# First MLP layer of the last two batches as a 2x2 block product with seven multiplications, placed behind attention

## The chip, the cores and the metric

The kernel runs on one core of a Trainium2 chip. The core has a matrix engine (TensorE, called PE in the profile), a vector engine (VectorE, DVE), an engine for activation functions (ScalarE, ACT), GpSimd (POOL) and an engine that mostly issues transfers (SyncE, SP). Each runs its own list of instructions in the written order and waits on semaphores for the others. Matrix products accumulate in PSUM (8 banks, each 512 fp32 wide in every partition); everything else lies in SBUF. The metric is the device time of one execution in microseconds; shown is the median of three runs.

## The reference

```python
def _attn_ref(q, k, v):                      # q, k, v: (8, 12, 448, 64)
    scores = scale * np.matmul(q, k.transpose(0, 1, 3, 2))
    attn = np.maximum(scores, 0.0) ** 2 / S
    return np.matmul(attn, v)
def _moe_ref(x, w_in, w_out):                # x: (3584, 768), w_in: (768, 2048), w_out: (2048, 768)
    h = x @ w_in
    g = 0.5 * h * (1.0 + erf(h * inv_sqrt2))
    return g @ w_out
# x is the attention output, heads side by side: 8 batches of 448 rows, 768 columns
```

So there are three parts: attention with squared ReLU for each batch and head, a first MLP layer with exact GELU, and a second MLP layer.

## The kernel before, in words

**Attention.** A batch has 12 heads in 3 groups `g` of 4. A QK step (`fn_qk`, L620) computes for one group 64 keys against 448 queries with four matmuls that use a quarter of the array each, into a PSUM buffer `ps` of two banks. A ReLU with scale brings it to bf16 in `a_sq`, on ACT (L632) or on DVE (L634), and DVE squares it (L641). Seven such steps make a group. Then an AV step (L680, 28 matmuls) multiplies with `v` into `pav`, and two copies (L384 on DVE, L386 on ACT) bring it to `xT`, the input of the MLP with features on partitions. `ps` and `pav` share a pool `w` of three two-bank buffers. An AV step is placed in the middle of the first four QK steps of the next group: two QK steps, the AV step, two QK steps, nothing else between them. The other three QK steps of a group stand together.

**First layer** (`add_f1`, L727). For each of 16 blocks `m` of 128 hidden units, six matmuls with a 128x128 weight tile of `win_sb` and 448 columns of `xT` accumulate in one PSUM bank of the pool `f` (two buffers); ACT applies GELU (L737) into the ring `h_sb`, which holds two batches. In batches 0 and 1 a few of these matmuls are 224 columns wide (half a batch).

**Second layer** (`add_group`, L834). Rows are taken in 14 groups of 256. The 2x2 block product (rows in two halves of 128, hidden units in two halves, output columns in two halves of 384) is formed with seven products instead of eight, of eight matmuls with 384 columns each. Four sums of `h_sb` blocks (L815, `s_sb`) and four differences of `wout_sb` blocks (L772, `t_sb`, made once by `add_tsums`) feed them; the partial results are added by DVE from PSUM (L868). The first 256 rows use plain products (`add_plain`, L929).

**Order.** The first 270 operations (attention of batches 0 and 1, the transposes, loads) follow a written list, `ORDER`. After it, the order on PE is fixed by the code at the end: for every batch `b` from 2 to 7 a stage of six slots takes the QK and AV steps, and between them "atoms" of the MLP. Stage `b` has the first layer of batch `b-1` and the groups that `GROUPS[b]` names, less the last three products of the last group, which are carried into the next stage (`CARRY`). So the stages hold different amounts of MLP work: two groups in stages 3, 4, 6 and 7, one in stages 2 and 5. Behind the attention of batch 7 come the rest of group 10, the first layer of batch 7, and groups 11 to 13. On ACT, DVE and SP a planner (`Scheduler`) chooses the order and, for ReLUs and copies, the engine, by its own costs, list positions and due times (`deadlines`).

**Transfers.** q and k of batches 2 to 7 are permuted by DVE (L463, L474) and transposed by seven transfers of the SP queue (L566 for kT, L575 for qT), which stand in one queue with the stores of the output rows (L795). POOL issues the loads; a small copy on POOL (`gate`, L587) waits for the transposes of batch `b+1` before the loads of `b+2` are issued. `wout_sb` is loaded in three pieces (L356).

Of the kernel before, what the change touches and what calls it, by code (L numbers as in the profile page):

```python
# [8 lines left out]
F32 = mybir.dt.float32  # L9
BF16 = mybir.dt.bfloat16  # L10
AF = mybir.ActivationFunctionType

B, H, S, D = 8, 12, 448, 64
# [37 lines left out]
SUM_BIAS = -0.3  # L51
TSUM_BIAS = 0.2
LEADS = {3: 8}
CARRY = 4
LAST = 256
PASSES = 2
NEAR = 0.5


def cols(half):  # L60
# [41 lines left out]
class Scheduler:  # L102
# [12 lines left out]
    def reset(self):  # L115
        self.free = {"PE": 6.0, "ACT": 2.6, "DVE": 1.0, "POOL": 1.25, "SP": 0.9}
        self.bufs = {name: [0.0] * n for name, n in self.buffers.items()}
        self.mode, self.dma = None, DMA_FREE
        self.landed = [0.0] * 8
        self.log = []  # L120
        for op in self.open:
            op.start = op.done = None

# [44 lines left out]
    def commit(self, est, op, eng, dur, lat):  # L168
        op.start = est
        if eng == "PE":  # L170
            self.mode = op.mode
            if est < self.COLD:
                dur, lat = 2 * dur, 2 * lat
        if isinstance(lat, tuple):
            t = max(self.dma, est + dur + 1.0)
            self.dma = t + lat[0] / 390e3
            op.done = self.dma + DMA_LAT
            self.landed += [op.done] * lat[1]
        else:
            op.done = est + lat  # L180
        self.free[eng] = est + dur
        for name in op.need:
            b = self.bufs[name]
            b[b.index(min(b))] = math.inf
        ends = [op.done] + [o.done for o in op.joint]
        if None not in ends:
            for name in op.frees:
                b = self.bufs[name]
                b[b.index(math.inf)] = max(ends)
        self.log.append((est, op, eng))  # L190

    def run(self, fixed):
# [11 lines left out]
    def deadlines(self):  # L204


        after = {id(o): [] for o in self.open}
        for o in self.open:
            for d in o.deps:
                if id(d) in after:  # L210
                    after[id(d)].append(o)
                elif isinstance(getattr(d, "op", None), Op):
                    after[id(d.op)].append(o)
        takers = {}
        for _, o, _ in self.log:
            for name in o.need:
                takers.setdefault(name, []).append(o)
        given = {}
        for _, o, _ in self.log:
            for name in o.frees:  # L220
                given.setdefault(name, []).append(o)
        for name, v in given.items():
            n = self.buffers[name]
            for x, o in enumerate(v):
                if x + n < len(takers[name]):
                    for y in [o] + list(o.joint):
                        after[id(y)].append(takers[name][x + n])
        self.late = {}
        t = math.inf
        order = sorted(self.log, key=lambda x: x[0])  # L230
        pe = [o for _, o, e in order if e == "PE"]
        ideal, at = {}, 0.0
        for o in pe:
            ideal[id(o)] = at
            at += o.engines[0][1]
        shift = pe[-1].start - ideal[id(pe[-1])]
        for est, o, e in reversed(order):
            t = ideal[id(o)] + shift if e == "PE" else est + 50.0
            for s in after[id(o)]:
                if id(s) in self.late:  # L240
                    t = min(t, self.late[id(s)] - (o.done - o.start))
            self.late[id(o)] = t

    def place(self, fixed):
# [36 lines left out]
def kernel(  # L281
# [100 lines left out]
    def copy(eng, dst, src):  # L382
        if eng == "DVE":
            V.tensor_copy(dst, src)  # L384
        else:
            A.copy(dst, src)  # L386

    def e_copy(n, psum=4):

        d = 0.07 + n / psum / 960  # L390
        return ("DVE", d, d + 0.12), ("ACT", 0.12 + 0.00074 * n, 0.24 + 0.00074 * n)
# [51 lines left out]
    def add_load(b, g0=0, g1=G):  # L443
        add_k(b, g0, g1)
        add_q(b, g0, g1)
        add_v(b, g0, g1)
# [56 lines left out]
    def old_T(b):  # L503
        return [o for (bb, *_), o in QK.items() if bb == b - 2]
# [56 lines left out]
    def add_T_dma(b, after):  # L561

        after = [list(x) for x in after]
        for g in range(G):
            def fn(e, g=g):
                nc.sync.dma_start_transpose(  # L566
                    get_T(b)[1][:, g].rearrange("p (i t) -> p i t", t=128), get_p()[1][:, g]
                )

            op = sch.add((("SP", 1.2, 3.0),), fn, [Pk[b, g]] + old_T(b) + after.pop(0))  # L570
            for i in range(NK):
                Tk[b, g, i] = (op, op)
        for c in range(NC):
            def fn(e, c=c):
                nc.sync.dma_start_transpose(get_T(b)[0][:, :, bass.ts(c, KC)], get_p()[0][:, c, :])  # L575

            op = sch.add((("SP", 1.2, 3.0),), fn, [Pq[b, g, c] for g in range(G)] + old_T(b) + after.pop(0))
            for g in range(G):
                Tq[b, g, c] = (op, op)

# [19 lines left out]
    def h_ring():  # L600

        if not hT:
            hT[0] = hpool.tile([128, KF, RING], BF16, tag="h", name="h_sb")
        return hT[0]
# [111 lines left out]
    def add_f1(b, m, half=None, bias=0.0):  # L716
# [36 lines left out]
            GL[b, m + x, half] = ge  # L753
        return op

    K2 = KF // 2
    quad = {
        (i, j): wout_sb[:, i * K2 : i * K2 + K2, j * ND : j * ND + ND]
# [5 lines left out]
    tsum[3] = quad[0, 1]  # L764
    SUMS = {}

    def add_tsums():

        def sub(n, c, a, b, deps):
            return sch.add(  # L770
                (("DVE", 0.95, 1.07),),
                lambda e: V.tensor_sub(tsum[n][:, c], a[:, c], b[:, c]), deps, bias=TSUM_BIAS,  # L772
            )

        for x, c in enumerate((slice(0, 4), slice(4, K2))):
            ld = list(ld_wout.values())
            t1 = sub(1, c, quad[0, 1], quad[0, 0], ld[: x + 1])
            t2 = sub(2, c, quad[1, 1], tsum[1], [t1] + ld)
            t4 = sub(4, c, quad[1, 0], tsum[2], [t2] + ld)
            SUMS[x] = [t1, t2, t4]  # L780
        for x, c in enumerate((slice(0, 4), slice(4, K2))):
            SUMS[x].append(sub(3, c, quad[1, 1], quad[0, 1], SUMS[x] + list(ld_wout.values()) + plain[:2]))
# [171 lines left out]
    def f1(b):  # L954
        return [(1.14, add_f1(b, m)) for m in range(KF)]
# [119 lines left out]
    class at_slot:  # L1075


        def __init__(self, b, n):
            self.key = plan[b][n][0][1]

        @property
        def done(self):
            return QK[self.key].done

    def at(b, n):
        return [at_slot(b, n)]

    stage = {}
    GROUPS = {2: (1,), 3: (2, 3), 4: (4, 5), 5: (6,), 6: (7, 8), 7: (9, 10), 8: (11, 12, 13)}
    add_load(3)  # L1090
    for b in range(2, B):
        add_steps(steps(b), dve=True)
        if b == 2:
            x1 = f1(b - 1)
            first_atoms, atoms = x1[:LEAD], x1[LEAD:]
            atoms += [(2.6, add_plain(t, n)) for n in (1, 0) for t in (0, 1)]
            add_tsums()
        else:
            atoms = carry + f1(b - 1)
        if b + 1 < B:  # L1100

            n = {2: 2, 3: 2}.get(b, 1)
            add_pk(b + 1, 0, G, after=at(b, n) + SUMS[0] + SUMS[1])
            add_pq(b + 1, 0, G, after=at(b, n) + SUMS[0] + SUMS[1])
            add_T_dma(b + 1, [at(b, n + (y >= 4)) for y in range(7)])
            if b + 2 < B:
                add_gate(b + 1)
                add_load(b + 2)
        x2 = [y for g in GROUPS[b] for y in add_group(g)]
        carry = x2[len(x2) - 7 + CARRY :]  # L1110
        stage[b] = atoms + x2[: len(x2) - 7 + CARRY]
    pe_q.extend(x[1] for x in first_atoms)
    for b, atoms in stage.items():
        for _ in range(LEADS.get(b, 0)):
            pe_q.append(atoms.pop(0)[1])
        total, gone = sum(x[0] for x in atoms), 0.0
        for n, slot in enumerate(plan[b]):
            for kind, x in slot:
                if kind == "FFN":
                    gone += atoms[0][0]  # L1120
                    pe_q.append(atoms.pop(0)[1])
                else:
                    pe_q.append(AV[x] if kind == "AV" else QK[x])
            while atoms and gone < total * (n + 1) / len(plan[b]) - 0.01:
                gone += atoms[0][0]
                pe_q.append(atoms.pop(0)[1])
    pe_q.append(AV[done])
    for _, o in carry + f1(B - 1) + [y for g in GROUPS[B] for y in add_group(g)]:
        pe_q.append(o)
    sch.run({"PE": pe_q, "POOL": pool_q})  # L1130
# [28 lines left out]
```

## Time and profile before

| | us |
|---|---|
| median of three runs (lowest, highest) | 377.79 (377.74, 378.91) |
| time of the profiled execution | 380.04 |
| its span, first to last instruction | 378.3 |
| PE busy in the span | 365.7 (97%) |
| DVE busy | 251.2 (66%) |
| ACT busy | 199.7 (53%) |
| first layer of batch 7, behind attention | 18.16 |

The page of the profile gives busy time for each engine, a row of 40 slices, the chain of work that ended last, groups of equal instructions with the mean duration of one, and the transfers. The granted TensorE clock is 0.999 of full speed. Matmuls are pipelined: a single row shows the time from a matmul's start to the end of its drain, so the spacing of a run of equal matmuls is (length of the run, less one duration) divided by (their number less one). In the timeline, start and length of a stretch of equal instructions stand in front, the idle time of the engine ahead of it and what released it in brackets behind.

### The profile page before, as it was taken

How to read it: one execution, taken by the hardware profiler on the slowest of the kernel's cores; microseconds unless marked ns; L12 is line 12 of the kernel's file. 1: busy time of each engine (PE TensorE's matmuls, PEld its weight loads, DVE VectorE, ACT ScalarE, POOL GpSimd, SP SyncE). 2: the span in 40 equal slices, each digit the busy share in tenths (PEclk: the TensorE clock that was granted, in tenths of full speed). 3: DMA queues.
4: the chain of work that ended last, by engine and by line, in shares of the span. 5: the costliest groups of instructions: out<-in, count | busy, mean ns of one | idle time of the engine just before them, and what ended most of it. 6: DMA issues, size and time to landing. Idle time of an engine off the chain costs nothing.

```text
span 378.3 us, 7922 instructions
## 1 busy us (share of the span) xinstructions
PE 365.7 (97%) x3341; PEld 202.1 (53%) x3341; DVE 251.2 (66%) x448; ACT 199.7 (53%) x306; POOL 45.7 (12%) x69
## 2 busy tenths in 40 slices
PE   8789999989999999999999999999999999999995
PEld 7566544445544455555555455555554455555663
DVE  3989981598836687863888648846885568601662
ACT  4988864666436754665456765565435653143000
POOL 8666400400002002002000020000000000000000
PEclk9999999999999999999999999999999999999999
DMA  9999999997399689987914894380203002200232
GB/s 175 196 202 206 200 170 119 165 205 133 88 146 184 111 123 177 209 121 112 164 57 111 121 141 79 98 132 2 83 2 86 0 3 83 66 19 2 83 85 83
DMA packets 69683, 42.93 MB, mean 113 GB/s; under 512 B 37776, under 2 KB 66192, under 8 KB 69648
## 3 DMA queue, kind: packets, MB, share of 16 engines
q0 software_dynamic: 30512, 22.47, 39.9%
q1 hardware_dynamic: 38768, 19.46, 25.2%
q8 instruction: 26, 0.43, 0.5%
q10 hardware_dynamic: 368, 0.51, 0.4%
q14 instruction: 9, 0.07, 0.1%
HBM read 45.61 MB, written 11.01 MB: 150 GB/s over the span
## 4 chain that ended last, share of the span: by engine, by line
PE 84%; DMA 7%; ACT 3%; issue 2%; DVE 1%; POOL 1%; SPq 1%; DVEq 0%; POOLq 0%; ACTq 0%
PE psh L727 35%; PE pso L834 32%; PE ps L620 8%; PE pav L680 6%; PE pso L929 3%; DMA wout_sb<-in_moe_w_out_dram 2%; DMA nk<-in_k_dram 2%; ACT a_sq L632 2%; DMA v_sb<-in_v_dram 2%; SPq L575 1%; DMA qT<-pq 1%; DVE a_sq L634 1%; ACT h_sb L737 0%; DVE a_sq L641 0%; POOL nk L418 0%
## 5 line engine op out<-in xcount | busy, mean ns | idle before, releaser
L727 PE MATMUL psh<-xT,win_sb 128*128 128x448 bf16 (+1 forms) x804 | 151.8, 344 | 0.1
L632 ACT ACTIVATE a_sq<-ps 128x896 bf16<-128x896 f32 (+1 forms) x133 | 114.6, 914 | 45.5 <-PE ps L620 45.4
L727 PEld LDWEIGHTS <-win_sb 128*128 128x128 bf16 x804 | 76.1, 98 | 71.4 <-issue 9.9
L737 ACT ACTIVATE h_sb<-psh 128x448 bf16<-128x448 f32 x128 | 69.9, 546 | 72.9 <-PE psh L727 71.7
L641 DVE TENSOR_TENSOR a_sq<-a_sq 128x896 bf16<-128x896 bf16 (+1 forms) x169 | 99.3, 617 | 10.4 <-ACT a_sq L632 9.3
L634 DVE TENSOR_SCALAR a_sq<-ps 128x896 bf16<-128x896 f32 x36 | 39.1, 1090 | 40.6 <-PE ps L620 40.4
L834 PEld LDWEIGHTS <-s_sb 128*128 128x128 bf16 x424 | 40.6, 98 | 28.2 <-issue 2.6
L620 PE MATMUL ps<-qT,kT 64*64 64x448 bf16 (+1 forms) x756 | 47.7, 336 | 4.3 <-ACT a_sq L632 1.3
L834 PEld LDWEIGHTS <-h_sb 128*128 128x128 bf16 x312 | 29.8, 98 | 22.3 <-issue 3.0
L680 PE MATMUL pav<-a_sq,v_sb 64*64 64x448 bf16 (+1 forms) x756 | 37.2, 330 | 1.3 <-issue 0.5
L834 PE MATMUL pso<-wout_sb,h_sb 128*128 128x384 bf16 x208 | 38.1, 326 | 0.0
L834 PE MATMUL pso<-t_sb,s_sb 128*128 128x384 bf16 x208 | 38.1, 326 | 0.0
L834 PE MATMUL pso<-wout_sb,s_sb 128*128 128x384 bf16 (+2 forms) x216 | 38.1, 320 | 0.0
L620 PEld LDWEIGHTS <-kT 64*64 64x64 bf16 x756 | 18.7, 105 | 27.0 <-issue 21.8
L868 DVE TENSOR_TENSOR osb<-pso,p_sb 128x384 f32<-128x384 f32 x39 | 21.8, 558 | 15.7 <-PE pso L834 13.9
L680 PEld LDWEIGHTS <-v_sb 64*64 64x64 bf16 x756 | 21.5, 107 | 13.4 <-issue 3.1
L384 DVE COPY p_sb<-pso 128x384 f32<-128x384 f32 x9 | 5.0, 558 | 26.0 <-PE pso L834 25.8
L386 ACT CAST xT<-pav 128x448 bf16<-128x448 f32 (+1 forms) x27 | 12.9, 506 | 15.8 <-DVE xT L384 15.0
L587 POOL COPY gate<-qT 128x4 bf16<-128x4 bf16 x5 | 0.9, 188 | 159.0 <-DMA qT<-pq 159.0
L834 PE MATMUL pso<-t_sb,h_sb 128*128 128x384 bf16 x104 | 19.0, 326 | 0.0
L868 DVE TENSOR_TENSOR osb<-pso,osb 128x384 f32<-128x384 f32 (+2 forms) x27 | 14.6, 543 | 5.4 <-PE pso L834 3.3
L815 DVE TENSOR_TENSOR s_sb<-h_sb 128x1024 bf16<-128x1024 bf16 x26 | 17.7, 682 | 0.0
(43 smaller groups left out, 163.8 us busy)
## 6 DMA issues: line engine op xcount, KB each, us to landing
nk<-in_k_dram POOLq DMA_DIRECT2D x5, 672.0 KB, 9.3
nq<-in_q_dram POOLq DMA_DIRECT2D x5, 672.0 KB, 12.0
v_sb<-in_v_dram POOLq DMA_DIRECT2D x5, 672.0 KB, 14.4
out_dram<-osb SPq DMA_DIRECT2D x8, 336.0 KB, 2.9
wout_sb<-in_moe_w_out_dram POOLq DMA_DIRECT2D x2, 1152.0 KB, 11.4
v_sb<-in_v_dram POOLq DMA_DIRECT2D x9, 224.0 KB, 8.3
out_dram<-osb SPq DMA_DIRECT2D x7, 288.0 KB, 2.9
out_dram<-osb SPq DMA_DIRECT2D x8, 240.0 KB, 3.0
```

The source lines that it names most:

```text
L386: A.copy(dst, src)
L620: nc.tensor.matmul(ps[64 * j : 64 * j + 64, e, x * w : x * w + w], kT[r, g, i * 128 + 64 * j : i * 128 + 64 * j + 64], qT[r, 2 * g + j, co ...
L632: A.activation(ar, ps, AF.Relu, scale=c_att)
L634: V.tensor_scalar(ar, ps, c_att, 0.0, op0=mybir.AluOpType.mult, op1=mybir.AluOpType.max,)
L641: V.tensor_mul(box["a2"][:, :, :used], ar, ar)
L680: nc.tensor.matmul(pav[0][o2 : o2 + 64, e, :w], vt[b][r, 2 * g + e, bass.ts(i, D)], box["a2"][r, e, o : o + w], start=(i == 0), stop=(i == ...
L727: nc.tensor.matmul(ph[:, x * n : x * n + n], win_sb[:, kd, bass.ts(m + x, 128)], xT[b][:, kd, c], start=(kd == 0), stop=(kd == KD - 1),)
L737: A.activation(h_ring()[:, m : m + nm, o + c.start : o + c.stop], box[0][:, :S].rearrange("p (x n) -> p x n", x=nm), AF.Gelu,)
L815: V.tensor_tensor(box["s", n], a(), b(), op=op)
L834: nc.tensor.matmul(box[bank][:, n0:n1], left()[:, kf], right[:, kf, n0:n1], start=bool(need) and kf == 0, stop=kf == K2 - 1, skip_group_ch ...
L868: V.tensor_add(out()[:, n0:n1], box[bank][:, n0:n1], other()[:, n0:n1])
L929: nc.tensor.matmul(box[0][:, :ND], h_ring()[:, kf, o : o + 128], wout_sb[:, kf, c], start=kf == 0, stop=kf == KF - 1,)
```

## The change

1. The first layer of batches 6 and 7 is no longer computed by `add_f1` but by `add_blocks`/`add_block`: a 2x2 block product. The 768 input features are two halves of three tiles (`K1 = 3`), the 2048 hidden units two halves of eight blocks (`M1 = 8`), the 448 rows of the batch two halves of 224 (`HS`). Seven products replace eight. Each product is three matmuls of 224 columns for a block `m`; two `m` share a PSUM bank, and two such pairs (`y`) share a two-bank buffer of the pool `w`. The three buffers of this pool hold the running partial sums "a", "b", "c".
2. New DVE work: sums of `win_sb` blocks (`add_wsums`, eight instructions, from stage 7 on; three of the four sums lie in buffers of the q and k loads, the fourth overwrites a block of `win_sb`), four sums of `xT` blocks per batch, and for every block of four `m` twelve passes from PSUM (one copy and five additions for each `y`). GELU then reads PSUM for one of the four results and SBUF for three.
3. The work of PE is laid out anew. The atoms of stages 2 to 7 are one list, `flow`, with the first layer of batches 1 to 5, the plain products and groups 1 to 8, spread evenly over the six stages. Behind the last AV step come: the block product of batch 6 woven with four products of group 9, the rest of group 9, group 10, the block product of batch 7 woven with four products of group 11, the rest of group 11, groups 12 and 13. `CARRY` is gone.
4. In the planner, an operation of `add_tsums` counts `wout_sb` as landed 2.0 us later than the planner's transfer model says (`Landed`, `LOAD_MARGIN`); the transposes get the mode "X", whose due times are spread 1.5 us apart in the queue (`QUEUE_STEP`); and buffers are matched to their takers in the order in which they really come free (`given`).

```diff
-CARRY = 4
+QUEUE_STEP = 1.5
+LOAD_MARGIN = 2.0
...
+            if e == "SP" and o.mode == "X":
+                t = min(t, queue - QUEUE_STEP)
...
-            op = sch.add((("SP", 1.2, 3.0),), fn, [Pk[b, g]] + old_T(b) + after.pop(0))
+            op = sch.add((("SP", 1.2, 3.0),), fn, [Pk[b, g]] + old_T(b) + after.pop(0), mode="X")
...
+        for m0 in (0, M1 // 2):
+            s1 = one(1, m0, add, part(0, 1), part(1, 1), [])
+            s2 = one(2, m0, sub, summed(1), part(0, 0), [s1])
+            s4 = one(4, m0, sub, part(1, 0), summed(2), [s2])
+            s3 = one(3, m0, sub, part(0, 0), part(0, 1), [s1] + done)
+            WS[m0] = {1: s1, 2: s2, 3: s3, 4: s4}
...
+        t1 = xsum(1, sub, x(0, 1), x(0, 0), [])
+        t2 = xsum(2, sub, x(1, 1), t(1), [t1])
+        t3 = xsum(3, sub, x(1, 1), x(0, 1), [])
+        t4 = xsum(4, sub, x(1, 0), t(2), [t2])
...
+                for z, m in enumerate(ms):
+                    w, mm = left(m)
+                    for k in range(K1):
+                        nc.tensor.matmul(
+                            bank[name][:, y, z * HS : z * HS + HS],
+                            w[:, k, bass.ts(mm, 128)],
+                            right()[:, k],
+                            start=first and k == 0 and z == 0,
+                            stop=k == K1 - 1,
+                            skip_group_check=not first or z > 0,
+                        )
...
+        p1 = product("a", plain(0, 0), x(0, 0), xs, True)
+        v1 = passed("a", "p", None, [p1], ("a",))
+        p6 = product("b", summed(2), t(2), [W[2], TS[2]], True)
+        v2 = passed("b", "t", "p", [v1, p6], ("a",))
+        p2 = product("a", plain(1, 0), x(1, 0), [v1])
+        c11 = gelu(lambda: ps("a"), 0, 0, [p2], ("w",))
+        p7 = product("b", summed(3), t(3), [v2, W[3], TS[3]])
+        v3 = passed("b", "u", "p", [p7], ("a",))
+        p5 = product("c", summed(1), t(1), [W[1], TS[1]], True)
+        c22 = passed("c", "u", "u", [v3, p5])
+        g22 = gelu(lambda: get("u"), 1, 1, [c22], ("a",))
+        p4 = product("b", plain(1, 1), t(4), [v3, TS[4]])
+        c21 = passed("b", "p", "p", [p4, v3, v2])
+        c21.frees = ("w",)
+        g21 = gelu(lambda: get("p"), 1, 0, [c21], ("a",))
+        p3 = product("c", summed(4), x(1, 1), [c22, W[4]])
+        c12 = passed("c", "t", "t", [p3])
+        c12.frees = ("w",)
+        g12 = gelu(lambda: get("t"), 0, 1, [c12], ("a",))
...
-            ld = list(ld_wout.values())
+            ld = [Landed(o) for o in ld_wout.values()]
...
-    GROUPS = {2: (1,), 3: (2, 3), 4: (4, 5), 5: (6,), 6: (7, 8), 7: (9, 10), 8: (11, 12, 13)}
+    F1B = {2: 1, 3: 2, 4: 3, 5: 4, 6: 5}
+    GROUPS = {2: (1,), 3: (2, 3), 4: (4, 5), 5: (6,), 6: (7, 8)}
...
+    add_wsums(at(B - 1, 1), [F1[B - 3, m, None] for m in range(KF)])
...
+    end = woven(add_blocks(B - 2), add_group(9), 4)
+    g10 = add_group(10)
+    end += g10 + woven(add_blocks(B - 1), add_group(11), 4)
+    end += add_group(12) + add_group(13)
...
+    share, gone, edge = sum(x[0] for x in flow) / (B - 2), 0.0, 0.0
...
+        start, edge = gone, edge + share
...
-    for _, o in carry + f1(B - 1) + [y for g in GROUPS[B] for y in add_group(g)]:
+    for _, o in end:
         pe_q.append(o)
```

In the order that results on PE, the products of a pair of `y` alternate: p1, p1, p6, p6, (group product), p2, p2, p7, p7, p5, p5, p4, (group product), p4, p3, p3, and once more for the other four `m`.

## The prediction

> **What bounds the kernel now.** I read the page's busy times first, then the end of the chain, then the timeline of PE where it stands still.
>
> ```profile
> PE 365.7 (97%) x3341; PEld 202.1 (53%) x3341; DVE 251.2 (66%) x448; ACT 199.7 (53%) x306; POOL 45.7 (12%) x69
> PE   8789999989999999999999999999999999999995
> ```
>
> PE is at 90% or more in all but five of the 40 slices: three at the start, the ninth (near 78 us), and the last. Nothing else is near its limit over the whole span. The end of the chain (start, length, what) agrees: behind the last AV step at 324.45 only PE work stands on it, and DVE closes it.
>
> ```profile
> 324.45 4.01 PE pso L834 x24
> 328.46 18.16 PE psh L727 x96
> 346.62 27.34 PE pso L834 x176
> 373.98 0.42 DVE osb L868
> ```
>
> So a matmul column saved is time saved, unless PE then waits for something. The timeline shows where it waits today, in three kinds of places.
>
> ```profile
> 74.54 0.96 DVE L772 TENSOR_TENSOR t_sb<-wout_sb 128x1536 bf16<-128x1536 bf16 x1 [4.05 <-DMA wout_sb<-in_moe_w_out_dram]
> 75.41 1.08 DVE L634 TENSOR_SCALAR a_sq<-ps 128x896 bf16<-128x896 f32 x1
> 75.59 0.38 PE L620 MATMUL ps<-qT,kT 64*64 64x448 bf16 x4
> 76.55 0.38 PE L620 MATMUL ps<-qT,kT 64*64 64x448 bf16 x4 [0.57 <-DVE a_sq L634]
> ...
> 79.15 0.38 PE L620 MATMUL ps<-qT,kT 64*64 64x448 bf16 x4 [0.43 <-DVE a_sq L634]
> ```
>
> First: DVE waits 4.05 us for `wout_sb`, and the ReLU behind it in its list is late, so PE's next QK step is late. Unhindered, two QK steps start 0.19 apart (8 matmuls last 0.57, 4 last 0.38). Here 75.59 to 76.55 is 0.77 too long, 78.34 to 79.15 is 0.62 too long, and the AV step between lasts 1.80 instead of 1.49: about 1.6 us.
>
> ```profile
> 112.42 0.57 PE L620 MATMUL ps<-qT,kT 64*64 64x448 bf16 x8 [0.63 <-issue]
> ```
>
> Second: the first QK step of batch 3 starts 0.7 late. The last transpose for it is issued at 109.63 and such a transpose lands 2.7 us later (page, transfers), at 112.3.
>
> ```profile
> 87.19 2.57 ACT L632 ACTIVATE a_sq<-ps 128x896 bf16<-128x896 f32 x3
> 88.43 0.36 PE L620 MATMUL ps<-qT,kT 64*64 64x448 bf16 x4
> 88.97 0.38 PE L620 MATMUL ps<-qT,kT 64*64 64x448 bf16 x4 [0.18 <-ACT a_sq L632]
> ...
> 262.44 0.92 ACT L632 ACTIVATE a_sq<-ps 128x896 bf16<-128x896 f32 x1 [2.33 <-PE ps L620]
> 262.63 1.09 DVE L634 TENSOR_SCALAR a_sq<-ps 128x896 bf16<-128x896 f32 x1
> 263.73 0.55 PE L620 MATMUL ps<-qT,kT 64*64 64x448 bf16 x8
> ```
>
> Third, the group boundary (two QK steps, AV step, two QK steps on three buffers): the fourth QK step needs the buffer that the second ReLU frees. At 88 both ReLUs are on ACT, one behind the other, and the fourth step starts 0.54 after the third: 0.35 lost. At 262 ACT and DVE take one each, and both steps run through. Of the 16 boundaries behind batch 2's first group, 5 have both on ACT, and these five are the ones that lose time (0.34, 0.39, 0.29, 0.47, 0.29; mean 0.36, sum 1.8). The other 11 (ACT, then DVE) lose nothing.
>
> **The cost of the change, part by part.**
>
> *Matmuls.* Removed: 2 x 96 of 448 columns. From the timeline of PE:
>
> ```profile
> 22.94 1.32 PE L727 MATMUL psh<-xT,win_sb 128*128 128x224 bf16 x12
> ...
> 328.30 18.32 PE L727 MATMUL psh<-xT,win_sb 128*128 128x448 bf16 x96
> ```
>
> 96 wide ones: (18.32 - 0.35)/95 = 0.189 each, so 192 x 0.189 = 36.3 us. Added: 2 batches x 4 blocks x 7 products x 6 = 336 of 224 columns. The row at 22.94 has just these, each with its own 128x128 weight load: (1.32 - 0.26)/11 = 0.0963, so 32.4 us. Saved: 3.9 us.
>
> Here a rule speaks against the change. The Trainium skill, "TensorE: Matmul & The Clock Gate", section "LDWEIGHTS (loading the stationary operand)", prices a load at columns / 1.2 ns, 107 ns for 128 columns, more than the 93 ns that 224 columns stream at 2.4 GHz; its section "Back-to-back issue gap" adds that in a stream of load and matmul pairs both set the spacing. At 107 ns the 336 would take an estimated 35.8 us and save 0.5. The trace has the very pair at 96 ns, so I take 3.9.
>
> *Switches of PE between attention and MLP* are 49 and 48 before and after: nothing.
>
> *Batch 2, the late `wout_sb`.* In the new order of DVE the waiting difference (L772) stands behind the ReLU and three squares instead of ahead of them. That ReLU can start near 72.0 (its QK steps start at 71.39), the squares end about 74.3, and the difference then starts at 74.54 without holding anybody up. The two ReLUs of the next boundary begin near 76.1 and free their buffers by 77.2, as the AV step ends. Gain 1.6 us; if the load landed over a microsecond later the gain would be gone.
>
> *First QK of batch 3.* There are now 48 first-layer matmuls between group 1 and it, 9.1 us, where 30 gave 5.7. On SP two stores stand between the kT and the qT transposes. The last permutation (L474) ends with group 1's last passes, four qT transposes at 1.3 us and 2.7 us of landing end about 6.3 us behind group 1: 2.8 us in hand. Gain 0.7.
>
> *Even stages.* Each has 27.6 us of MLP work by the planner's weights, where four had 36.4 and two about 25 to 27. More ReLUs go to ACT (141 full-size ones instead of 131) and copies of `xT` to DVE. At the 16 boundaries both ReLUs are now on ACT at 10, DVE then ACT at 5, ACT then DVE at 1. The 10 cost 3.6 us at 0.36, 1.8 more than before. The 5 have no row: between nothing (the first ReLU on DVE would end 0.2 before its buffer is asked for) and 0.36 each (1.8); nearest are the 11 mixed ones at zero, so I take 0.2 in all.
>
> *Transfers in thinner stages.* Groups 1 to 10 keep their stores, four transfers a group; those of 9 and 10 move behind SP's last transpose. For batch 6, five transposes stand behind group 5's stores: 0.8 of passes, 0.9 of stores, 5 x 1.3 and 2.7 make about 10 us, while PE has 12.5 us of steps and first layer before it needs them. The loads gated by them are 12 us (q) from being in and asked for 13 us into the stage. All hidden; each is within 1 to 3 us of showing.
>
> *The woven tail.* From the last AV step to group 10, PE has 168 x 0.0963 + 7 x 1.30 = 25.3 us. DVE has 24 passes of 448 fp32 columns. No such addition is in the trace; between 0.558 (L868, 384 columns) and 0.621 (L384, 448 columns from PSUM) I take the latter, being of the same width. With five weight sums at 0.95, five L868 at 0.558, two L815 at 0.68 and an `xT` copy: 24 x 0.621 + 4.75 + 2.8 + 1.4 + 0.6 = 24.5 us. Rows overlap by some 0.09 in close order (328.50 to 328.97 for one of 0.56), so nearer 21. It fits, and the alternation of two `y` leaves each dependent product about 0.9 us: p4 starts 1.7 us behind its p7 and needs 0.2 + 0.62. The tightest wait is group 10's second product, which needs sums of the last GELU of batch 6; about 0.6 in hand. ACT has 16 GELUs of 0.55 in this time. I put down 0.2, in a range of 0 to 3. The three weight sums and some `xT` sums in stage 7, about 4 us, lie in DVE's free 14 of 40.5 us.
>
> Sum: -3.9 - 1.6 - 0.7 + 1.8 + 0.2 + 0.2 = -4.0. On the profiled span, 378.3 - 4.0 = 374.3. The profiled execution took 380.04, 1.7 more than its span, but the median of the runs is 377.79, 0.5 below the span; the difference carries over: **373.8 us**. A change of 0.3% (1.1 us) is about what a measurement tells from none.
>
> **Rivals.**
> - *The boundaries don't lose more*: the ten on ACT find it idle more often, or the waits are absorbed. Then -5.8 to -6: about 371.8. Against it: all five such boundaries lose today, in every kind of stage.
> - *The thin stages and the tail wait more*: mixed boundaries cost 0.36 too (+1.6), or transposes or sums come 1 us late in one or two places: 375.0 to 376.6. For it: DVE's copies and the small margins above.
> - *Half-width products aren't half price* (107 ns): only about -0.6, near 377.2. The trace's 96 ns speak against it, though at 12 to 24 in a row.
> - *Slower: VectorE bounds the woven blocks.* Both blocks would have to lose over 5 us together, 2.6 each. DVE's 24.5 us has to become 27.9, so the 20 additions have to take over 0.79 us instead of 0.62. At 0.85 each block loses 3.8 and the time is about 381. An addition of a PSUM and an SBUF operand at this width isn't in the trace; at 384 columns it takes no longer than a copy (both 0.558), which speaks against it.
>
> **Chances.** Forecast (372.6 to 375.0) 0.52; boundaries no worse, or better (under 372.6) 0.20; more waits (375.0 to 376.6) 0.18; no visible change 0.05; slower 0.05. Range: leaving out a tenth at each side, 371.5 to 376.3. Faster by over 0.3%: 0.52 + 0.20 + 0.18 = 0.90.
>
> **What would show it.** PE's rows of L870: 96 ns apart, 336 of them, and no idle time over 0.2 us in front of them. No idle PE at 75 to 80 us and none ahead of batch 3's first QK step. Ten idles of PE behind an ACT ReLU in stages 2 to 7, about 0.36 each. DVE's additions (L904) of 0.6. The prediction is wrong if matmuls of the block product start over 100 ns apart, if PE waits for DVE in the woven blocks, or if QK steps wait for transposes at the start of batch 4, 5, 6 or 7.

## The result, and the profile after

| | before | after |
|---|---|---|
| median, us | 377.76 | 376.0 (375.88 to 376.11) |
| ratio of the runs, 95% interval | | 0.9946 [0.9927, 0.9965] |
| profiled execution, us | 380.04 | 375.98 |
| its span, us | 378.3 | 374.2 |
| PE / DVE / ACT busy, us | 365.7 / 251.2 / 199.7 | 363.0 / 284.3 / 200.9 |

The kernel is faster by 1.8 us by the medians, by 2.0 us (1.3 to 2.8) by the ratio. Run again beside the later experiments it gave the same ratio, 0.9946 [0.9929, 0.9962]. The forecast was 4.0 us: about half came. The span, on the other hand, is where the prediction put it (374.3 against 374.2). The two don't fit together because the profiled execution of before was itself 2.3 us longer than its median, a point that the experiments take up first. That the spans agree to 0.1 us is in part luck: the tail cost 1.5 us more than predicted, the boundaries 0.9 less, the matmuls saved 0.2 more, and PE began stage 2 0.3 us earlier (65.32 against 65.63).

The page of the changed kernel; columns are busy us, share and instructions of each engine.

```profile
span 374.2 us, 8324 instructions
PE 363.0 (97%) x3485; PEld 215.4 (58%) x3485; DVE 284.3 (76%) x517; ACT 200.9 (54%) x301; POOL 46.0 (12%) x69
```

PE is still the bound, with 144 more matmuls and less time in them; DVE has 33 us more. The timeline of the changed kernel in the same places as before (start, length, instructions, idle time before them):

```profile
74.31 0.95 DVE L974 TENSOR_TENSOR t_sb<-wout_sb 128x1536 bf16<-128x1536 bf16 x1
75.28 0.57 PE L623 MATMUL ps<-qT,kT 64*64 64x448 bf16 x8
75.69 1.49 PE L683 MATMUL pav<-a_sq,v_sb 64*64 64x448 bf16 x28
...
77.01 0.55 PE L623 MATMUL ps<-qT,kT 64*64 64x448 bf16 x8
...
113.09 0.57 PE L623 MATMUL ps<-qT,kT 64*64 64x448 bf16 x8
...
122.35 1.73 ACT L635 ACTIVATE a_sq<-ps 128x896 bf16<-128x896 f32 x2 [0.92 <-PE ps L623]
...
123.64 0.87 PE L623 MATMUL ps<-qT,kT 64*64 64x448 bf16 x8
```

The waits at 75 to 80 us and ahead of batch 3 are gone: eight QK matmuls last 0.55 to 0.57 with nothing idle in front. At 122 both ReLUs of a boundary are on ACT, and the eight matmuls behind the AV step last 0.87 instead of 0.55 as at 77. Measured from start to start (four QK matmuls in close order take 0.19), each of the ten boundaries with both ReLUs on ACT loses 0.285 us, to within 0.001; the six mixed ones lose nothing.

New are five waits in the woven blocks. In the timeline of the block of batch 7, the products p7, p5 and p4 and the additions behind p7:

```profile
330.47 1.31 PE L870 MATMUL pb<-xs,win_sb 128*128 128x224 bf16 x12
...
331.62 1.31 PE L870 MATMUL pb<-xs,ws 128*128 128x224 bf16 x12
331.82 2.84 DVE L904 TENSOR_TENSOR part<-pb,part 128x448 f32<-128x448 f32 x5 [0.18 <-PE pb L870]
333.03 0.73 PE L870 MATMUL pb<-xs,win_sb 128*128 128x224 bf16 x6
```

The first product p7 has ended by 331.2, but the first addition starts at 331.82, as the second p7 leaves the array (331.78). And the first p4 doesn't start when p5 has streamed (332.77) and its own addition is done (332.4), but at 333.03, when both additions of the pair are. In all four such places the first p4 starts 0.05 us behind the end of the second addition. That is 0.26 us of idle PE, four times. The fifth wait is in the chain of the changed kernel (start, length, what):

```profile
296.33 2.30 DVE part L904 x4
298.64 0.87 DVE ws L794
299.50 0.54 DVE part L904
300.09 4.18 PE pb L870 x42
```

The second p4 of the pair, at 300.09, waits for the pass over the first p4's result (299.50), which stands behind a weight sum on DVE: 0.68 us.

### The profile page after: what moved, and what is told of

Its sections match the earlier page's. It is cut to its first block, busy times and chain, and to the rows that moved or that the text cites. A ratio compares the mean times of both kernels' runs of the same rounds, so it can differ in the third digit from the quotient of the medians.

```text
span 374.2 us, 8324 instructions
## 1 busy us (share of the span) xinstructions
PE 363.0 (97%) x3485; PEld 215.4 (58%) x3485; DVE 284.3 (76%) x517; ACT 200.9 (54%) x301; POOL 46.0 (12%) x69
## 4 chain that ended last, share of the span: by engine, by line
PE 84%; DVE 6%; ACT 4%; issue 2%; DMA 2%; POOL 1%; DVEq 0%; ACTq 0%; POOLq 0%
PE pso L1036 32%; PE psh L730 29%; PE ps L623 8%; PE pb L870 7%; PE pav L683 4%; ACT a_sq L635 4%; PE pso L1131 3%; DVE a_sq L644 3%; DVE part L904 2%; DMA nk<-in_k_dram 2%; DVE a_sq L637 1%; DVE xT L387 0%; DVE kT L387 0%; PE tp L517 0%; ACT xT L389 0%
## 5 line engine op out<-in xcount | busy, mean ns | idle before, releaser
L635 ACT ACTIVATE a_sq<-ps 128x896 bf16<-128x896 f32 (+1 forms) x143 | 122.8, 914 | 57.5 <-PE ps L623 57.5
L730 PE MATMUL psh<-xT,win_sb 128*128 128x448 bf16 (+1 forms) x612 | 114.2, 342 | 0.1
L740 ACT ACTIVATE h_sb<-psh 128x448 bf16<-128x448 f32 x96 | 52.5, 547 | 34.3 <-PE psh L730 34.0
L623 PE MATMUL ps<-qT,kT 64*64 64x448 bf16 (+1 forms) x756 | 48.5, 336 | 3.1 <-ACT a_sq L635 0.7
L637 DVE TENSOR_SCALAR a_sq<-ps 128x896 bf16<-128x896 f32 x26 | 28.2, 1088 | 28.5 <-PE ps L623 28.1
L387 DVE CAST xT<-pav 128x448 bf16<-128x448 f32 (+1 forms) x44 | 24.3, 582 | 5.5 <-PE pav L683 4.9
L904 DVE TENSOR_TENSOR part<-pb,part 128x448 f32<-128x448 f32 x40 | 23.1, 618 | 6.3 <-PE pb L870 6.2
L913 ACT ACTIVATE h_sb<-part 128x448 bf16<-128x448 f32 x24 | 13.3, 577 | 18.4 <-DVE part L904 18.3
```

Source lines behind the costliest of these rows:

```text
L623: nc.tensor.matmul(ps[64 * j : 64 * j + 64, e, x * w : x * w + w], kT[r, g, i * 128 + 64 * j : i * 128 + 64 * j + 64], qT[r, 2 * g + j, co ...
L635: A.activation(ar, ps, AF.Relu, scale=c_att)
L637: V.tensor_scalar(ar, ps, c_att, 0.0, op0=mybir.AluOpType.mult, op1=mybir.AluOpType.max,)
L730: nc.tensor.matmul(ph[:, x * n : x * n + n], win_sb[:, kd, bass.ts(m + x, 128)], xT[b][:, kd, c], start=(kd == 0), stop=(kd == KD - 1),)
L740: A.activation(h_ring()[:, m : m + nm, o + c.start : o + c.stop], box[0][:, :S].rearrange("p (x n) -> p x n", x=nm), AF.Gelu,)
L904: V.tensor_add(get(to), ps(name), get(other))
```

## The experiments

Three questions were open: where half of the forecast went, whether the block product or the new layout gains, and whether the waits can be taken away.

**1. Was the profiled execution of before a usual one?** The kernel before, unchanged, profiled again.

> The kernel before, unchanged, profiled once more. Theory A: the late w_out wait at 75 to 80 us (1.6 us of PE) and the late first QK step of batch 3 (0.7 us) belong to the one profiled execution that took 380.04 us; a usual execution of 377.8 us has a span near 376.0 us and neither of the two waits (under 0.3 us together). Rival B: the waits stand in every execution, and the profiled one was longer elsewhere: span near 376.0 us with about 2.3 us of idle PE in those two places.

It took 378.67 us with a span of 376.9. Its timeline:

```profile
73.04 0.96 DVE L772 TENSOR_TENSOR t_sb<-wout_sb 128x1536 bf16<-128x1536 bf16 x1 [3.03 <-DMA wout_sb<-in_moe_w_out_dram]
...
76.84 0.38 PE L620 MATMUL ps<-qT,kT 64*64 64x448 bf16 x4
77.66 0.38 PE L620 MATMUL ps<-qT,kT 64*64 64x448 bf16 x4 [0.43 <-DVE a_sq L634]
```

Here `wout_sb` is there at 73.04 instead of 74.54, and PE loses 0.6 us in one place instead of 1.6 in three. The wait ahead of batch 3 is there, 0.8 us. From the first QK step of batch 3 on, both traces of the kernel agree to 0.02 us in every stage and in the end part; all that differs lies ahead of it (46.79 against 45.86 us for stage 2, and 0.5 us before). So neither theory holds whole: the wait ahead of batch 3 stands in both traces, while the landing of `wout_sb` differs from one to the other. The load itself was not slower in the first. POOL issues it behind `gate`, which waits for transposes (POOL's timeline, first profile, then this one):

```profile
65.56 0.19 POOL L587 COPY gate<-qT 128x4 bf16<-128x4 bf16 x1 [21.16 <-DMA qT<-pq]
65.79 1.65 POOL L356 DMA_DIRECT2D wout_sb<-in_moe_w_out_dram  x2
...
63.71 0.19 POOL L587 COPY gate<-qT 128x4 bf16<-128x4 bf16 x1 [19.31 <-DMA qT<-pq]
63.95 1.65 POOL L356 DMA_DIRECT2D wout_sb<-in_moe_w_out_dram  x2
```

The load was issued 1.85 us later in the first profile and then took 8.7 us to land, against 9.1 here. In the eleven traces of this case `gate` starts between 63.3 and 66.0 us, latest in the two executions that lie 2.3 us above their kernel's median (the first of the kernel before, and that of experiment 5's last kernel). Why the transposes ahead of it land sooner or later is open.

**2. The late load alone.** The kernel before with the margin on the planner's landing time, and the changed kernel without it. On DVE the one difference of `wout_sb` moves behind or ahead of a ReLU and its squares; in the kernel before, near 250 us, a GELU on ACT and a square on DVE also change places with a neighbour, and the stages from batch 3 on stay equal to 0.02 us.

```diff
-            ld = list(ld_wout.values())
+            ld = [Landed(o) for o in ld_wout.values()]     # Landed adds 2.0 us to done
```

> The kernel before with one thing of the change: the planner counts w_out as landed 2.0 us later, so the second t_sb difference stands behind a ReLU and three squares on DVE. Theory A: no change, 377.8 us within 0.3, since the load is usually in time. Rival B: 1.6 us faster, about 376.2 us.

> The changed kernel with the margin set to 0: only the one t_sb difference goes back ahead of the ReLU on DVE. Theory A: 376.0 us within 0.3 like the changed kernel. Rival B: 1.6 us slower, about 377.6 us.

The kernel before with the margin: ratio 0.9984 [0.9972, 0.9997] to the kernel before, 0.6 us faster (0.1 to 1.1). The changed kernel without it: 0.9970 [0.9959, 0.9981] instead of 0.9946, so 0.9 us slower; its trace shows 0.96 us of idle PE at 76 us again (the larger part, in its timeline):

```profile
77.84 0.57 PE L623 MATMUL ps<-qT,kT 64*64 64x448 bf16 x8 [0.62 <-DVE a_sq L637]
```

The gain is real, and by the ratios 0.6 to 0.9 us, not the 1.6 of the first profile. In the kernel before it comes mostly from the long executions: by the medians it is only 0.2 (377.51 against 377.70), but nine of 45 runs without the margin took over 378.2 us, and none of 20 with it. Rival B was too large in both kernels. Theory A was too small in the changed kernel; in the kernel before its 0.3 holds by the medians and not by the ratio.

**3. Block product or layout.** The changed kernel with plain products in the same places.

```diff
-    add_wsums(at(B - 1, 1), [F1[B - 3, m, None] for m in range(KF)])
...
-    end = woven(add_blocks(B - 2), add_group(9), 4)
-    g10 = add_group(10)
-    end += g10 + woven(add_blocks(B - 1), add_group(11), 4)
+    end = f1(B - 2) + add_group(9)
+    end += add_group(10)
+    end += f1(B - 1) + add_group(11)
```

> The changed kernel with the first layer of batches 6 and 7 as plain products of 448 columns in the same places behind attention, no weight sums, no x sums; everything ahead of the end of attention as in the changed kernel. If the block product saves 3.9 us of matmuls and gives back 1.7 us in waits of the woven blocks, this takes 376.0 + 2.2 = 378.2 us. Rival: the block product gains nothing on balance and the gain comes from the new layout of the stages: 376.0 us or less.

Ratio to the kernel before 1.0013 [0.9997, 1.0028], median 378.41. Against 0.9946 the block product is worth 2.5 us (forecast 2.2); by the traces, from the last AV matmul to the end of the last matmul it is 82.08 against 79.65, 2.4 us. Stage 7 takes 0.3 of that back (38.38 us in the plain version, 38.70 in the changed kernel), since the plain version has no weight and `xT` sums on DVE there and one boundary less with both ReLUs on ACT; 2.1 is left by the traces. The layout with its other planner changes, margin included, gains nothing by itself.

**4. The waits in the woven blocks.** One group product of each half block is moved from between the two p4 to ahead of both.

```diff
-            while k < n and (k + 0.5) / n < gone / tx:
-                out.append(y[k])
-                k += 1
+            if i in (3, 9, 17, 23):
+                out.append(y[(3, 9, 17, 23).index(i)])
```

> The changed kernel with the second and fourth woven group product of each block moved from between the two p4 to ahead of both. Theory C: the two halves y share a buffer and are waited for as one, so p4 needs both passes that follow the second p7 (0.2 + 1.16 us), and two p5 (1.15 us) don't cover them; with a group product of 1.3 us more between, all five waits go: 1.7 us faster than the changed kernel, 374.3 us. Rival D: VectorE is behind with its list (weight sums, group sums), so the waits move elsewhere: within 0.5 us of 376.0 us.

374.56 us, ratio 0.9907 [0.9892, 0.9921]: 1.6 us faster than the changed kernel beside it by the medians (376.14), 1.5 by the ratios (1.7 forecast). All five waits are gone (77.96 us for the end part instead of 79.65). The same place in the timeline:

```profile
296.34 1.31 PE L870 MATMUL pb<-xs,ws 128*128 128x224 bf16 x12
296.55 2.31 DVE L904 TENSOR_TENSOR part<-pb,part 128x448 f32<-128x448 f32 x4 [0.29 <-PE pb L870]
297.49 1.46 PE L1036 MATMUL pso<-t_sb,s_sb 128*128 128x384 bf16 x8
...
298.79 1.31 PE L870 MATMUL pb<-xs,win_sb 128*128 128x224 bf16 x12
```

DVE still sits idle before the additions and waits for PE, so it isn't behind (Rival D). The group product fills 297.49 to 298.79, and all twelve p4 matmuls run through. Theory C holds; separate buffers for the two `y`, which would test it from the other side, were not tried.

**5. The boundaries.** First ReLU of every group from batch 2 on to ACT, second to DVE, in the changed kernel; then together with experiment 4; then in the kernel before.

```diff
+            if blocks[0][0] >= 2 and blocks[0][2] == 1:
+                eng = eng[1:]            # DVE
+            elif blocks[0][0] >= 2 and blocks[0][2] == 0:
+                eng = eng[:1]            # ACT
```

> The changed kernel with the first ReLU of every group from batch 2 on bound to ACT and the second to DVE, so that all 16 boundaries have the mixed order. Theory E: a boundary with both ReLUs on ACT costs 0.285 us, a mixed one nothing: 10 x 0.285 = 2.85 us faster than the changed kernel, 373.1 us. Rival F: VectorE has no room for ten ReLUs of 1.09 us more, squares come late and AV steps wait: under 1 us faster, 375 us or more.

> Both edits together. If theories C and E hold, the gains add: 376.0 - 1.7 - 2.85 = 371.5 us. If VectorE is short of room (D, F): 374 us or more.

> The kernel before with the same binding of ReLUs (first of a group to ACT, second to DVE, from batch 2 on) and nothing else of the change. Its five boundaries with both ReLUs on ACT lose 0.34, 0.39, 0.29, 0.47 and 0.29 us in the trace. Theory E: all five go, 1.8 us, about as much as the whole change gained: ratio 0.995. Rival F: a boundary wait taken away comes back as another wait of the stage, since VectorE holds five ReLUs more: under 0.5 us, ratio above 0.9985.

The changed kernel with the binding: 372.95 us, ratio 0.9873 [0.985, 0.9896], 3.2 us faster than the changed kernel by the medians and 2.8 by the ratios (2.85 forecast; Theory E). None of the 16 boundaries has both ReLUs on ACT; the trace shows one boundary wait left, 0.35 us, and no 0.68 us wait in the first block, since the planner's list for DVE came out otherwise: 2.85 + 0.68 - 0.35 makes the 3.2. A boundary now:

```profile
121.83 0.92 ACT L635 ACTIVATE a_sq<-ps 128x896 bf16<-128x896 f32 x1 [0.92 <-PE ps L623]
122.02 1.09 DVE L637 TENSOR_SCALAR a_sq<-ps 128x896 bf16<-128x896 f32 x1 [1.51 <-PE ps L623]
...
123.12 0.55 PE L623 MATMUL ps<-qT,kT 64*64 64x448 bf16 x8
```

Both edits together: 372.47 us, ratio 0.985 [0.9835, 0.9865], the fastest kernel here, 5.6 us under the kernel before, but 1.0 us above the forecast of 371.5, and 1.1 short of the sum of the two measured gains (1.6 and 3.2). In that sum 0.68 is counted twice: it is the long wait in the first block, which each edit takes away by itself. The remaining waits of the woven blocks are gone (77.96 us for the end part, 78.98 with the binding alone), and in this trace 0.8 us comes back elsewhere. The first QK step of batch 4 waits for a transpose (timeline of this kernel, PE):

```profile
140.15 0.57 PE L623 MATMUL ps<-qT,kT 64*64 64x448 bf16 x8 [0.97 <-DMA qT<-pq]
```

With the binding, the six permutations of q stand later on DVE than in the changed kernel (131.13 to 132.42 us here; four of the six from 127.01 there). With the binding alone the order of work up to this place is the same, and the wait in its trace is 0.2; so the binding opens the step to this wait, and how long it is differs from one execution to the next.

In the kernel before, the same edit gained nothing: 378.36 us, ratio 1.0009 [0.9999, 1.0019]. Theory E fails there and Rival F holds. The five waits of 0.29 to 0.47 went, and three came in their place, 1.2, 1.1 and 0.5 us. The first of them in its timeline:

```profile
87.32 0.57 PE L620 MATMUL ps<-qT,kT 64*64 64x448 bf16 x8
...
87.47 0.95 DVE L776 TENSOR_TENSOR t_sb<-wout_sb,t_sb 128x1536 bf16<-128x1536 bf16 x1
...
88.33 0.69 DVE L819 TENSOR_TENSOR s_sb<-h_sb 128x1024 bf16<-128x1024 bf16 x1
88.94 1.82 DVE L776 TENSOR_TENSOR wout_sb<-wout_sb 128x1536 bf16<-128x1536 bf16 x2
...
90.42 0.38 PE L620 MATMUL ps<-qT,kT 64*64 64x448 bf16 x4 [1.02 <-ACT a_sq L632]
90.67 0.69 DVE L819 TENSOR_TENSOR s_sb<-s_sb,h_sb 128x1024 bf16<-128x1024 bf16 x1
...
91.28 1.08 DVE L634 TENSOR_SCALAR a_sq<-ps 128x896 bf16<-128x896 f32 x1
```

The ReLU bound to DVE stands behind four differences and sums of the second layer and one more; its QK step was at 87.3, it starts at 91.28. PE takes the next buffer that an ACT ReLU frees, a microsecond late. At the other two places the ReLU on DVE (139.19, 150.62) also stands behind sums or passes of the second layer. This execution was the longest of its 13 (380.63 us), with `wout_sb` late again, but that is not what delays DVE here: it had caught up, and waited for ACT just before 86.92. The binding helps only where the list of DVE has room at that point.

**6. The changed kernel once more**, beside experiments 4 and 5.

> The changed kernel, unchanged, beside the others on the same chip: 376.0 us, ratio 0.995, span near 374.2 us, with the same five waits of PE in the woven blocks (four of 0.26 us, one of 0.68 us) and ten of 0.285 us at the group boundaries.

Median 376.14, ratio 0.9946, and the fifteen waits are all there. Its profiled execution was the longest of its four, 376.91 us with a span of 375.1, and shows what the even stages are exposed to (timeline):

```profile
214.92 0.57 PE L623 MATMUL ps<-qT,kT 64*64 64x448 bf16 x8 [0.41 <-DMA qT<-pq]
...
222.03 1.00 DVE L466 COPY pk<-nk 128x896 bf16<-128x896 bf16 x3 [1.86 <-DMA nk<-in_k_dram]
...
226.72 1.30 DVE L477 COPY pq<-nq 112x512 bf16<-112x512 bf16 x6 [1.96 <-DMA nq<-in_q_dram]
...
229.61 0.38 PE L623 MATMUL ps<-qT,kT 64*64 64x448 bf16 x4 [0.41 <-DVE a_sq L637]
```

The transposes of batch 6 land 0.4 to 0.5 us late, the loads behind them as well, DVE stands twice for nearly 2 us before its permutations, and a ReLU behind them holds up PE: 1.0 us together. In the first profile of this kernel the same steps ran through.

## Why the prediction was half right

It was right in sign, and 376.0 lies in its range, in the case "the thin stages and the tail wait more" (375.0 to 376.6) and not in the likeliest one. By its own steps:

| step | predicted | measured | from |
|---|---|---|---|
| matmuls | -3.9 | -4.1 | 336 at 0.0958 us from start to start, 32.2 against 36.3 |
| late `wout_sb` | -1.6 | -0.6 to -0.9 | experiment 2, by the ratios |
| first QK of batch 3 | -0.7 | -0.4 to -0.8 | wait in three traces of the kernel before and its margin version (0.70, 0.80, 0.41), none after |
| boundaries, both ReLUs on ACT | +1.8 | +1.1 | 10 x 0.285 against 1.8 |
| mixed boundaries | +0.2 | 0 | no wait at the six |
| woven tail | +0.2 | +1.7 | 4 x 0.26 + 0.68; 1.5 to 1.6 by experiment 4 |
| sum | -4.0 | -2.3 to -3.0 | against -1.8 (medians), -2.0 (ratio) |

- **The woven tail** is the term that was mis-sized. The step "the alternation of two `y` leaves each dependent product about 0.9 us: p4 starts 1.7 us behind its p7 and needs 0.2 + 0.62" failed. It treated the two `y` as separate. They share one two-bank buffer, and in the built program the first of two passes waits for both products and the first of two products for both passes. So the pair needs 0.2 + 1.16 us, and 0.05 more until p4 starts, 1.41 us in all, and has two p5 of 0.575 to cover it, 1.15. The difference, 0.26, is the size of the four waits. The range of 0 to 3 did hold it. The load of DVE, on which the step spent most of its words, was sized well: the additions took 0.618 (forecast 0.62), and only the fifth wait (0.68) has to do with other work on DVE: a weight sum stood ahead of one pass. All the same, a sign that the prediction had named as showing it wrong, PE waiting for DVE in the woven blocks, did come.
- **The conversion** "the median of the runs is 377.79, 0.5 below the span; the difference carries over" failed. A profiled execution takes some 1.8 us more than its span (380.04 and 378.3, 375.98 and 374.2), so a usual run of the kernel before has a span near 376.0, and the profile in hand was 2.3 us longer than usual. That was to be seen from the table: the profiled execution lay above the highest run shown. A gain that rests on a wait for a transfer, as that for `wout_sb`, has then to be taken as a sample. The prediction said that the gain would be gone if the load landed later; it didn't ask what was left of it if the load landed earlier.
- **The boundaries** were read rightly: which ones wait followed from the order of the two programs. The mean of 0.36 was too high, since ACT was still busy ahead of three of the five in the kernel before, with a GELU at two (0.39 and 0.47) and a copy at one (0.34); the other two lost 0.29.
- **The rule on weight loads** (the Trainium skill, "TensorE: Matmul & The Clock Gate", section "LDWEIGHTS (loading the stationary operand)": columns / 1.2 ns, so an estimated 107 ns for 128 columns) would have left 0.5 us of the 4.1, less than the woven blocks lose in waits. The block product's 336 matmuls start 95 to 96 ns apart with a load each (98 ns for one), as the twelve of the first profile did; the measurement decides, and over long runs.
- **Transfers in thinner stages** were "hidden, each within 1 to 3 us of showing". For batch 6 its own figures (0.8, 0.9, 5 x 1.3 and 2.7) make 10.9 us and not about 10, so 1.6 of the 12.5 were left. Some waits do show in some executions: at batch 6 in experiment 6, another of the signs it had named, and at batch 4 in experiment 5, with a changed list. In the first profile of the changed kernel there is none.
- **What is left of the sum.** The terms make 0.3 to 1.2 us more than the measured gain. Between the second trace of the kernel before and the first of the changed kernel they account for all of it: -4.1 - 0.6 - 0.8 + 1.1 + 1.7 = -2.7, and the spans are 376.9 and 374.2. The changed kernel's 374.2 is also the span of its usual run, but a usual run of the kernel before, near 376.0, is 0.9 shorter than that trace. So the rest is to be looked for in the kernel before, whose usual run presumably has smaller waits than either trace shows; which ones is open, since no such run was traced.

## What to carry to other kernels

Before a wait in a profile is counted as gain, compare the profiled execution's own time with the runs: what it was longer by lay, here, in waits behind transfers. Where two halves of work share a buffer, the slack between dependent steps is that of the pair: count from the end of the second producer to the end of the second consumer, and put unrelated work of that length between them. And count in the order of the built program which engine frees each buffer at each tight place: that count told here exactly which boundaries would wait, ten and not six, though not how long (0.285 us each, not 0.36). Binding two ReLUs of each group gained about as much (2.8 to 3.2 us, 0.68 of it from a wait elsewhere) as seven products instead of eight (2.5 us), but only where the other engine's list had room for it.

## What the runs showed of the hardware

- From one execution to the next the same program repeats to 0.02 us a stage where it waits for no transfer: stages 3 to 7 of the kernel before took 35.77, 45.69, 37.25, 45.69 and 47.29 us in one trace and the same within 0.01 in another. All of the difference between these two executions was in front, among loads and transposes; in the changed kernel (experiment 6) 1.0 us of it came at batch 6, again behind transfers.
- The same load landed 1.5 us apart in two executions (74.5 and 73.0), not because it was slower (8.7 and 9.1 us from issue to landing) but because its issue waited for transposes that landed later (issue at 65.79 and 63.95).
- A 128-column weight load took 98 ns by its row, and the 336 matmuls of 224 columns with one such load each still started 95 to 96 ns apart.
- A DVE addition of 448 fp32 values from PSUM and SBUF took 0.618 us, a DVE copy of the same width out of PSUM 0.618 too: the second operand cost nothing here.
